# Another string of ordering rules for the planner of a fused attention and MLP kernel

## The chip, the cores and the metric

The kernel runs on one core of one Trainium2 chip. The metric is the device time in microseconds (us). A profile is one execution, recorded by the hardware profiler. A core has a matrix engine (TensorE, here PE; its weight loads are PEld), VectorE (DVE), ScalarE (ACT), GpSimd (POOL) and SyncE (SP), which issues DMAs. Each engine works through its own queue in order, and engines wait for each other by semaphores.

## The reference

All activations are bf16, with one batch, 2048 tokens of width 640, 32 query heads of width 20 that share one key and one value head, and an MLP of width 1728.

```python
xn = _layernorm(x, axis=-1)
q  = (xn @ wq).reshape(B, S, 32, 20).transpose(0, 2, 1, 3)
k, v = xn @ wk, xn @ wv
p  = softmax(einsum("bhqd,bkd->bhqk", q, k) * 20 ** -0.5)
A  = einsum("bhqk,bkd->bhqd", p, v).transpose(0, 2, 1, 3).reshape(B, S, 640) @ wo
out = x + A + silu(xn @ w1) @ w2
```

## The kernel before

**A planner writes the queues.** The program isn't written out by hand. `build` describes each instruction as an `Op` with its engine, an assumed duration (`occ`), what it reads and writes and a priority, and a greedy scheduler (`Sched`) then steps a clock for each engine. At each step the engine whose clock is lowest picks one of the ops that could start (`step_pe` for PE, `step_other` for the rest), and `commit` fixes it at the next place of that engine's queue. `emit` turns the resulting orders into instruction streams and adds the semaphore waits that the data need. Nothing of the planned times goes into the program, only the orders; but which bank of PSUM, which buffer and which engine an op uses is decided on the way too, so one other choice early changes everything that follows.

**Attention.** Heads are taken in eight groups of four and queries in four blocks of 512, which makes 32 head groups ("groups", `NGR`). For each group and each of the 16 tiles of 128 keys there are four blocks of scores of 128 x 512, one for each head, 2048 in all. The score matmuls (L1078) contract over only 20 of 128 rows, so up to four of them run side by side in four row strips of the array: a score set. A block fills one of the eight PSUM banks. Its exponential is taken in one of two ways:
- ACT takes two or three blocks at a time, from adjoining banks, with one instruction of 1024 or 1536 columns (L1166). `plan` chooses the banks and `make_s_act` makes the score set.
- DVE approximates it: L1409 adds a constant, clamps and converts to int16, which read as bf16 is a power of two that is linear between the powers. Two further copies of the tile, shifted by constants (the "shifts", four blocks at a time), smooth the result. They run on POOL (L1448) or on DVE (L1453), as `dve_advance` finds POOL loaded. Four blocks make a batch, opened by `claim`.

The product of p with v (p.v; L1201) runs as four column strips side by side, a set of four matmuls, and adds up in one PSUM bank for the group; a batch of DVE's has three sets, one for each shift. An extra column of v sums p. At the end of a group the bank is copied to U (L1250, or added to an earlier part, L1249), the sums are turned into reciprocals and spread by DMAs, POOL multiplies (L860) and DMAs pack the result into oT. The last two groups take a shorter way: sums by PE (L999), spread by PE (L1017), a product on DVE (L1026).

**The other matrix work ("misc").** `fill_misc` lists it in a fixed order: the q projections, the hidden layer of the MLP (h; its tanh is ACT's L773, its product DVE's L776), and for each query block the output jobs, which add the MLP's second layer and the attention's projection (out; for the last query block y, with a remainder fin). All of them run as sets of four column strips through `col_mm` (L447), 512 columns for q and h and 320 for out and y; a matmul of a job may instead run as one or four row strips beside a score set (`row_mm`, L454). PE can't run row strips and column strips at once, so it goes back and forth between bursts of scores and bursts of sets.

**What PE does next** is decided in `step_pe`: `pe_candidates` gathers what could start now (a score set for ACT "s", one for DVE "d", p.v from ACT "p" or from DVE "pd", misc "m" or "l", a row strip "r" and others), and the order of kinds is written as a list that depends on the mode that PE is in and on how far things lag. If nothing can start within 250 ns or so, `filler` puts in matmuls on zeros (L1725).

**The rules.** About thirty numbers steer these choices; they stand in `BASE` and are read as `ru.name`. `RULES` has one letter for each of some forty variants that change one or two of these numbers. `PLAN` is a string with one letter for each 10 us of PE's planned time:

```python
if sc.t["pe"] >= piece * PIECE:          # PIECE = 10000.0 ns
    ru.__dict__.update(BASE)
    ru.__dict__.update(RULES[rule(piece)])
    piece += 1
```

Some of the letters: `need` and `hold` (m, P, n, Q) say how long ahead of ACT's running dry a score set is placed and whether it waits for three adjoining banks; `stay` (o, J, K) lets PE go on with its sets until so many ns before ACT runs dry; `slack`, `want` (q, w, v) say when banks are kept for DVE; `open` (p, t) how many batches DVE may have open; `pj` (z, C, E) when a shift goes to POOL; `rows`, `half` (A, B, G, H, I) when matmuls run as row strips; `hold2` (x, F) whether a second misc job may hold a bank; `leadmax` (k, l) how far misc may run ahead of the attention; a changes nothing.

Of the kernel before, what the change touches and what calls it, by code (L numbers as in the profile page):

```python
# [105 lines left out]
RULES = dict(a={}, b=dict(keep=0.0), c=dict(lagp=3), d=dict(lagp=5), e=dict(lagp=0), f=dict(patience=200.0), g=dict(dwant=0.0),  # L106
             h=dict(zcap=4), i=dict(zcap=3), j=dict(homes=0), k=dict(leadmax=-1.0, lead=-1.0), l=dict(lead=0.08, leadmax=0.1),
             m=dict(need=740.0), n=dict(hold=0.0), o=dict(stay=640.0), p=dict(open=1), q=dict(slack=560.0), r=dict(hungry=1000.0), s=dict(claim=9), t=dict(open=3), u=dict(claim=4), v=dict(want=2), w=dict(slack=850.0), x=dict(hold2=4), y=dict(bnd=0), z=dict(pj=-1e9), A=dict(rows=0), B=dict(rows=2, rowmin=2), C=dict(pj=2000.0), D=dict(openlag=3), E=dict(pj=8000.0), F=dict(hold2=3), G=dict(rows=1), H=dict(half=0), I=dict(half=3), J=dict(stay=560.0), K=dict(stay=720.0), P=dict(need=560.0), Q=dict(hold=120.0), L=dict(uopen=3), M=dict(uopen=4), N=dict(uopen=5), O=dict(uopen=0))
PLAN = "acbtJKazNvhaJvxvixrrnrKzDDnQDmoqvknpfLBGvDPmoJdftFQdkttaQBBoknQEaoz"


def rule(n):
    return PLAN[n] if n < len(PLAN) else "a"
PACE = 1.0
# [2059 lines left out]
```

## Time and profile before

| | us |
|---|---|
| median of 3 runs | 691.98 |
| lowest and highest run | 691.73, 692.18 |
| the profiled execution | 691.7 |
| its span, first to last instruction | 689.9 |
| granted PE clock, mean | 1.00 |

The profile's page gives each engine's busy time as a share of the span. Views of the trace give busy time in stretches of the span, groups of instructions by line and shape (count | total busy, mean of one | idle time of the engine ahead of them, and what ended it), who waited for whom (total, times, longest), an engine's instructions in order of time (equal ones that follow each other are merged; the second number is how long the merged run lasted), and the chain of waits: the work that ended last, followed back from the last instruction. Ends of matmuls are modelled, so a busy PE may still have small gaps. L followed by a number is a line of the kernel. A count of matmuls is of single ones; four column strips make a set.

### The profile page before, as it was taken

To read this page: it belongs to the slowest core of one execution; us is meant where nothing else is said; L and a number is where in the kernel's file an instruction comes from. 1 tells how busy PE (TensorE), PEld (TensorE's weight loads), DVE (VectorE), ACT (ScalarE), POOL (GpSimd) and SP (SyncE) were. 2 spreads that over 40 slices of the span, in tenths; PEclk is the share of its full clock that TensorE was granted. 3 is DMA by queue.
4 is the path that set the end of the run, shared out by engine and by line. 5 is a ranking of instruction groups with operands and counts; after the bars stand their busy time and mean duration, and the time that the engine had idled before them with its cause. 6 is when DMAs were issued, how large, how long until landed. Compare 5 with 4: busy or idle time off the path is not lost.

```text
span 689.9 us, 22614 instructions
## 1 busy us (share of the span) xinstructions
PE 676.4 (98%) x9870; PEld 234.4 (34%) x9873; DVE 594.7 (86%) x1017; ACT 665.9 (97%) x726; POOL 583.9 (85%) x351
## 2 busy tenths in 40 slices
PE   8999999999999999999999999999999999999998
PEld 5432222322233333323233333322232333333345
DVE  7899989988998867898988888798988889989973
ACT  6999999999999999999999999999999999999990
POOL 6668899898988889898899899989889998888860
PEclk9999999999999999999999999999999999999999
DMA  7753221122221232321212223222222202223201
GB/s 217 178 180 42 20 20 15 33 35 30 18 28 12 31 40 30 69 34 17 33 14 30 29 31 40 23 65 29 29 19 22 22 18 32 31 23 68 23 7 41
DMA packets 34241, 28.97 MB, mean 42 GB/s; under 512 B 15486, under 2 KB 29662, under 8 KB 34142
## 3 DMA queue, kind: packets, MB, share of 16 engines
q1 hardware_dynamic: 33854, 27.20, 25.7%
q8 instruction: 77, 1.26, 0.8%
q10 hardware_dynamic: 288, 0.33, 0.1%
q14 instruction: 22, 0.18, 0.1%
HBM read 11.09 MB, written 2.62 MB: 20 GB/s over the span
## 4 chain that ended last, share of the span: by engine, by line
PE 76%; ACT 16%; DVE 4%; POOL 1%; SPq 1%; DMA 1%; issue 1%; DVEq 0%; ACTq 0%
PE psall L1201 26%; PE psall L1078 25%; PE psall L447 23%; ACT sbt L1166 14%; DVE sbt L1409 1%; ACT sbt L773 1%; POOL sbt L1448 1%; SPq L706 1%; DMA sbt<-sbt 0%; PE psall L621 0%; DVE sbt L563 0%; PE psall L734 0%; DVE sbt L607 0%; PE psall L1725 0%; DVE sbt L565 0%
## 5 line engine op out<-in xcount | busy, mean ns | idle before, releaser
L1166 ACT ACTIVATE sbt<-psall 128x1024 bf16<-128x1024 f32 (+1 forms) x654 | 643.0, 1156 | 2.3 <-PE psall L1078 2.1
L1448 POOL TENSOR_SCALAR sbt<-sbt 128x2048 int16<-128x2048 int16 x275 | 521.7, 1897 | 70.4 <-DVE sbt L1453 22.4
L1409 DVE TENSOR_SCALAR sbt<-psall 128x512 int16<-128x512 f32 x676 | 441.8, 685 | 64.4 <-PE psall L1078 60.1
L1078 PE MATMUL psall<-sbt 32*128 32x512 bf16 x2048 | 269.2, 384 | 4.3 <-ACT sbt L1166 1.6
L1201 PE MATMUL psall<-sbt 128*32 128x512 bf16 x3400 | 264.8, 384 | 0.6 <-POOL sbt L1448 0.4
L447 PE MATMUL psall<-sbt 128*32 128x320 bf16 (+3 forms) x3792 | 227.6, 332 | 2.5 <-DVE sbt L1409 0.8
L1078 PEld LDWEIGHTS psall<-sbt 32*128 32x128 bf16 x2048 | 71.4, 91 | 238.8 <-ACT sbt L1166 172.7
L447 PEld LDWEIGHTS psall<-sbt 128*32 128x32 bf16 (+1 forms) x3792 | 82.4, 95 | 82.7 <-issue 44.7
L1201 PEld LDWEIGHTS psall<-sbt 128*32 128x32 bf16 x3400 | 70.1, 94 | 114.5 <-issue 71.0
L1453 DVE TENSOR_SCALAR sbt<-sbt 128x2048 int16<-128x2048 int16 x63 | 48.6, 784 | 0.7 <-PE psall L1201 0.6
L860 POOL TENSOR_TENSOR sbt<-sbt 128x512 bf16<-128x512 f32 x30 | 38.2, 1274 | 7.2 <-DVE sbt L1453 5.5
L776 DVE SCALAR_TENSOR_TENSOR sbt<-sbt,psall 128x512 bf16<-128x512 bf16 x52 | 35.6, 684 | 5.2 <-ACT sbt L773 2.6
L773 ACT ACTIVATE sbt<-psall 128x512 bf16<-128x512 f32 x52 | 37.6, 723 | 0.1
L1250 DVE COPY sbt<-psall 128x512 f32<-128x512 f32 x31 | 21.2, 683 | 1.1 <-PE psall L1201 1.0
L454 PE MATMUL psall<-sbt 32*128 32x320 bf16 x70 | 21.3, 305 | 0.0
L1725 PE MATMUL psall<-sbt 128*32 128x256 bf16 (+1 forms) x228 | 14.4, 355 | 1.2 <-DVE sbt L487 1.2
L693 DVE TENSOR_SCALAR sbt<-psall 128x512 bf16<-128x512 f32 x20 | 13.6, 680 | 0.4 <-PE psall L447 0.4
L903 DVE SCALAR_TENSOR_TENSOR sbt<-psall,sbt 128x320 bf16<-128x320 f32 x24 | 11.6, 485 | 2.1 <-PE psall L447 1.6
L572 POOL TENSOR_TENSOR sbt<-sbt 128x2 f32<-128x2 f32 x8 | 5.7, 709 | 8.7 <-DVE sbt L570 8.3
L585 POOL TENSOR_SCALAR sbt<-sbt 128x640 bf16<-128x640 bf16 x12 | 10.4, 874 | 1.5 <-DVE sbt L577 1.5
L919 DVE SCALAR_TENSOR_TENSOR sbt<-psall,sbt 128x320 f32<-128x320 f32 x8 | 3.9, 486 | 8.0 <-PE psall L447 8.0
L1725 PEld LDWEIGHTS psall<-sbt 128*32 128x32 bf16 x228 | 7.0, 114 | 4.5 <-issue 1.6
(64 smaller groups left out, 117.9 us busy)
## 6 DMA issues: line engine op xcount, KB each, us to landing
sbt<-sbt SPq DMA_DIRECT2D x120, 64.0 KB, 3.9
sbt<-in_A_x_dram SPq DMA_DIRECT2D x28, 160.0 KB, 4.0
sbt<-sbt SPq DMA_DIRECT2D x213, 20.0 KB
out_dram<-sbt SPq DMA_DIRECT2D x14, 160.0 KB, 2.0
sbt<-in_B_w_dram SPq DMA_DIRECT2D x1, 2160.0 KB, 13.4
sbt<-in_B_w_dram SPq DMA_DIRECT2D x1, 2080.0 KB, 8.1
sbt<-sbt SPq DMA_DIRECT2D x75, 8.0 KB
sbt<-in_A_wq_dram SPq DMA_DIRECT2D x1, 800.0 KB, 5.9
```

The costliest lines, as they stand in the source:

```text
L447: ins = pe.matmul(ps[j * SLOT:(j + 1) * SLOT, b * BANK + off:b * BANK + off + n], w[:, j * SLOT:(j + 1) * SLOT], x, start=start, stop=stop ...
L454: return pe.matmul(ps[0:w.shape[-1], b * BANK:b * BANK + n], w[k], x[k], start=start, stop=stop, tile_position=(r * SLOT, 0))
L773: t = Op("act", lambda a: a.activation(t_buf[0:rows, ts, :], bk(job.bank, 0, QW, rows=rows), AF.Tanh, scale=0.5), t_act(512), ACT_END, pre ...
L776: u = Op("dve", lambda v: v.scalar_tensor_tensor(out=hT[par][0:rows, fk, :], in0=t_buf[0:rows, ts, :], scalar=1.0, in1=bk(job.bank, 0, QW, ...
L860: nm = pool(lambda e: e.tensor_tensor(oU[:, us, :], U_sb[:, us, :], Rrep, ALU.mult), 1356.0, POOL_END, pre=[uc] + lc + pack_op.get(divmod( ...
L1078: return pe.matmul(bk(b), kT_rep[i * SLOT:(i + 1) * SLOT, kt * P:(kt + 1) * P], qT[i * SLOT:(i + 1) * SLOT, g % NQ, :], start=True, stop=T ...
L1166: return a.activation(Ebuf[:, es * QW:es * QW + w], ps[:, buf[0] * BANK:buf[0] * BANK + w], AF.Exp, scale=ESCALE)
L1201: ins = pe.matmul(ps[i * SLOT:(i + 1) * SLOT, ub * BANK:ub * BANK + QW], lhsT, rhs, start=(first and k < HG), stop=(last and k >= len(lst) ...
L1409: p1 = Op("dve", lambda v: v.tensor_scalar(z16[:, i * QW:(i + 1) * QW], bk(job.bank), ZBIAS, 0.0, ALU.add, ALU.max), t_dve(QW) + 2.0, DVE_ ...
L1448: op = pool(lambda v, t=t, j=j, zin=zin: v.tensor_scalar(t.bitcast(I16), zin, float(SHIFT[j]), 1.0, ALU.add, ALU.mult), POOL_SHIFT, POOL_E ...
L1453: op = dve(lambda v, t=t, j=j, zin=zin: v.tensor_scalar_add(t.bitcast(I16), zin, float(SHIFT[j])), t_dve(N, 4), prio=SPRIO - 0.01 * j, **args)
L1725: ins = pe.matmul(ps[i * SLOT:(i + 1) * SLOT, ub * BANK:ub * BANK + n], zero_t[:, 0:SLOT], zero_t[:, 0:n], start=fresh, stop=fresh, tile_p ...
```

## The change

Only the string of letters changes. Its length stays 67, the first three letters stay, and of the other 64 two agree by place.

```diff
-PLAN = "acbtJKazNvhaJvxvixrrnrKzDDnQDmoqvknpfLBGvDPmoJdftFQdkttaQBBoknQEaoz"
+PLAN = "acbgxnoQpQJvpnaQodtxzpvEoQJBJoaodpJqQaDqJovpkBrnvxBxQJBfaaooHoatano"
```

Behind the first three letters the new string has o (stay=640) ten times, a (the base alone) seven times, Q (hold=120) and J (stay=560) six times each, p (open=1) five times, and x (hold2=4), n (hold=0), v (want=2) and B (rows=2, rowmin=2) four times each. The old one has v five times, t (open=3), a, n, D (openlag=3), Q and o four times each, and twenty other letters up to three times each. The planner runs with these while the program is built, so the change shows in the program as other orders in the queues and as other counts of a few kinds of instructions:

| | before | after |
|---|---|---|
| ACT L1166, 1024 / 1536 / 512 columns | 590 / 64 / 0 | 594 / 61 / 1 |
| DVE L1453, shifts | 63 | 65 |
| POOL L1448, shifts | 275 | 273 |
| DVE L1249, partial copies of U | 6 | 4 |
| PE L1725, matmuls on zeros | 228 | 188 |
| PE L447, 512 / 320 columns | 1476 / 2208 | 1468 / 2196 |
| PE L454, row strips | 70 | 78 |
| PE, bursts of one kind | 1322 | 1331 |

All other kinds have the same counts. The first instruction that stands elsewhere comes after about 30 us of the planned time; behind it every queue is ordered anew. PE's queue ends like this (a row is a run of equal matmuls):

```
before                         after
L1078 128x512 x3               L1078 128x512
L1201  32x512 x56              L454  128x320
L447   32x320 x80              L447   32x320 x36
L999  128x4   x4               L1201  32x512 x4
L1017  32x128 x16              L447   32x320 x72
L447   32x320 x68              L999  128x4   x4
                               L1017  32x128 x16
then in both: L447 32x128 x20, 32x384 x20, 32x128 x4, 32x384 x12, 32x128 x8,
32x384 x4, 32x128 x4, 32x512 x24, 32x256 x36, 32x512 x12
```

Ahead of that, ACT's queue ends with seven instructions of 1536 columns before, and with nine of 1536 and one of 512 after.

## The prediction

> **What bounds the kernel now.** I read the table of engines first, then busy time in six stretches of 100 us, then ACT's instructions, then the end of the chain of waits.
>
> ```profile
> span 689.9 us, 22614 instructions
> ...
> PE 676.4 (98%) x9870; PEld 234.4 (34%) x9873; DVE 594.7 (86%) x1017; ACT 665.9 (97%) x726; POOL 583.9 (85%) x351
> ```
> ```profile
> core 0: us, PE busy (x) PEld busy (x) DVE busy (x) ACT busy (x) POOL busy (x), PEclk, DMA share, GB/s
> ...
> 536.00:636.00 100.00, 99.47 (x1570) 35.00 (x1568) 90.10 (x148) 99.79 (x105) 88.03 (x51) 1.00 0.25 34
> sum 600.00, PE 593.90 PEld 191.89 DVE 527.98 ACT 599.32 POOL 532.86; mean PE 98.98 PEld 31.98 DVE 88.00 ACT 99.89 POOL 88.81
> ```
>
> Two engines are full at once. From 36 to 636 us ACT lacks 0.7 us of being always busy and PE 6.1 us. To see which sets the end, I take ACT's own pace and compare it with the stage.
>
> ```profile
> L1166 ACT ACTIVATE sbt<-psall 128x1024 bf16<-128x1024 f32 x590 | 563.9, 1118 | 2.3 <-PE psall L1078 2.1
> ...
> L1166 ACT ACTIVATE sbt<-psall 128x1536 bf16<-128x1536 f32 x64 | 95.1, 1509 | 0.0
> ```
> ```profile
> 13.59 1.92 ACT L1166 ACTIVATE sbt<-psall 128x1024 bf16<-128x1024 f32 x2
> ...
> 22.64 7.44 ACT L1166 ACTIVATE sbt<-psall 128x1024 bf16<-128x1024 f32 x8 [0.48 <-PE psall L1078]
> 29.88 0.69 ACT L631 ACTIVATE sbt<-psall 128x512 bf16<-128x512 f32 x1
> ...
> 664.06 9.52 ACT L1166 ACTIVATE sbt<-psall 128x1536 bf16<-128x1536 f32 x7
> ```
>
> Eight exponentials of two banks start at 22.64 and the next instruction at 29.88: 0.905 us each, although one lasts 1.118 (neighbours overlap by 0.21). Seven of three banks end 9.52 us after the first starts: without that overlap 1.33 each. The difference, 0.427, is one bank; one bank alone takes 0.905 - 0.427 = 0.48. So ACT needs 590 x 0.905 + 64 x 1.33 + 57 x 0.48 = 646.5 us (57 one-bank instructions at L773, L744 and L631, by the program). It had from 13.59 to 664.06 + 9.52 = 673.58: 660.0 us. Only 13.5 us, 2%, are stalls. The time is therefore the 13.6 us ahead, ACT's work with its stalls, and the 16.3 us from the last exponential to the end. PE comes next: what it hasn't finished when ACT ends is paid for one to one in those 16.3 us.
>
> ```profile
> 662.06 0.55 PE psall L1201 x8
> ...
> 664.72 0.98 PE psall L1201 x16
> ...
> 671.11 0.33 PE psall L1078 x3
> 671.43 3.21 PE psall L1201 x56
> 674.65 2.72 PE psall L447 x80
> 677.36 0.98 PE psall L999 x8
> 678.35 1.01 PE psall L1017 x32
> 679.36 6.60 PE psall L447 x200
> ```
>
> This is the end of the chain. Four column matmuls run side by side as one set. Sixteen against eight of L1201 give (0.98 - 0.55) / 2 = 0.215 us for a set of 512 columns, and 0.55 - 2 x 0.215 = 0.12 for the change of mode before a burst. Eighty of L447 give 2.72 / 20 = 0.136 for a set of 320. After the last score set (671.11) PE still has 14 sets of p.v, 20 sets of 320 columns, the sums and spreads of the last head group, and 200 matmuls more: PE ends with a backlog.
>
> **The change part by part.** The work stays the same; the string picks other rules for 62 of 67 pieces of 10 us of planned time, all from 30 us on, and the planner lays the queues anew. I counted both programs' instructions in queue order and priced the differences.
>
> ACT: 594 exponentials of two banks for 590, 61 of three for 64, one of one bank for none; 1372 blocks of scores in both, and 169 batches for DVE in both. 4 x 0.905 - 3 x 1.33 + 0.48 = **+0.1 us**.
>
> DVE and POOL: two shifts of z move from POOL (275 to 273) to DVE (63 to 65), and two partial copies of U fall away (6 to 4).
>
> ```profile
> L1453 DVE TENSOR_SCALAR sbt<-sbt 128x2048 int16<-128x2048 int16 x63 | 48.6, 784 | 0.7 <-PE psall L1201 0.6
> ```
> ```profile
> 672.30 1.90 POOL L1448 TENSOR_SCALAR sbt<-sbt 128x2048 int16<-128x2048 int16 x1 [2.04 <-PE psall L1201]
> ```
>
> POOL has 2 x 1.90 = 3.8 us less to do, DVE at most 2 x 0.784 = 1.6 us more. Both lie under ACT, whose share of the span is 97% against their 86 and 85%; I cost them at nothing. Without that cover DVE's part would be 1.6.
>
> PE's order at the end, which decides: after the last score set the new queue holds 1 set of p.v for 14. Of 320 columns it holds 9 sets ahead of that p.v, 18 between it and L999, and none behind L1017; before these were 0, 20 and 17 (68 of the 200). What follows (the final products, their DVE sums, two stores) is the same list. The tail from the last exponential's end is then, against 16.3: p.v 674.65 - 673.58 = 1.07 becomes one set and its hand-over, 0.3 (-0.8); two sets of 320 fewer (-0.3); 17 fewer (-2.3). Sum **-3.4 us**. The 17 sets also covered the way from L1017 over DVE's product to the first matmul that needs it. Ten other sets (128 and 384 columns, by width 5 x 0.05 + 5 x 0.16 = 1.1 us) still stand there; DVE's two products were through 0.5 us after L1017, so I cost the lost cover at nothing:
>
> ```profile
> 678.99 0.86 DVE L1026 TENSOR_TENSOR sbt<-sbt,psall 128x256 bf16<-128x256 f32 x2 [0.40 <-PE psall L1017]
> ```
>
> This has to be earned earlier: 13 x 0.215 + 10 x 0.136 = 4.2 us more PE work stands before the last score set. Its sources: PE's fill matmuls, which compute nothing, go from 21 sets to 11 behind the prologue.
>
> ```profile
> 521.65 0.60 PE L1725 MATMUL psall<-sbt 128*32 128x512 bf16 x8
> ...
> 530.70 0.28 PE L1725 MATMUL psall<-sbt 128*32 128x256 bf16 x4
> ```
>
> Between these two stand nine bursts of fill, ten sets: the old order has nothing else for PE there, while its tail holds work. The new order has three sets left in the last third of the run. Eight sets of 512 and two of 256 fewer free 8 x 0.215 + 2 x 0.11 (half of it) = 1.9 us. The last score set may also come later, because its exponential has one bank and not three: 1.33 - 0.48 = 0.85, with the 0.1 above 0.95. Nine more bursts cost 9 x 0.12 = 1.1; five more sets (two of 512, three of 320) done as row matmuls inside score sets save 0.8. So 4.2 - 1.9 - 0.95 + 0.3 = **1.6 us** must come out of PE's 6.1 us of idle time. Bounds: if all comes from idle time it costs nothing; if none does, ACT's stalls grow by 1.6. I take the middle, +0.8, since some idle time is waiting for banks that ACT holds. Burst by burst the orders look alike: after 30 us, 60 stretches from one exponential's scores to the next hold over 0.2 us more PE work than the exponential before them lasts; in the new order 45. I see no reason for more stalls, and allow 1.5 us either way (a tenth of the 13.5).
>
> Sum against the profiled execution, 691.7 (span 689.9 and 1.8 around it): +0.1 - 3.4 + 0.8 = -2.5, so 689.2. The median is 0.3 higher (691.98): **689.5 us**, own range 687.2 to 691.8 (0.8 and 1.5 to either side).
>
> [...]
>
> **The rivals.**
>
> ```profile
> PEld psall L1078 <- ACT sbt L1166: 172.7, 479, 0.8
> ...
> PEld psall L1201 <- POOL sbt L1448: 12.5, 49, 0.5
> ```
>
> (a) *No denser.* Score loads wait 479 times for ACT's banks; where PE waits so, work can't be packed more tightly, and more work between score sets only makes ACT wait. For: PE is busy for 99.5 of the 100 us from 536 on. Against: 1.9 us are fills, visibly free. Its price: stalls rise by a quarter, 3.4 us, and the tail's gain is given back: 691.98 + 0.1 - 3.4 + 3.4 = 692.1, no change.
>
> (b) *POOL late at the end; slower.* By the row above, POOL's last shift ends at 674.2, 0.6 us after the last exponential, and the last p.v sets wait for it. In the new order every p.v set from DVE's batches stands ahead of the last score set, so that shift must end some 2 us before the last exponential does. If it comes as it did, 2.6 us late, PE stands with the last score set behind it; one shift more makes 2.6 + 1.9 = 4.5: 689.5 + 4.5 = 694.0. It is slower than before from that second shift on. For: p.v waits for POOL 49 times even now. Against: POOL has 3.8 us less to do, and nine three-bank exponentials end the new order (seven before), so DVE's last batch is some 2.7 us earlier.
>
> (c) *The clock falls.* With ten fill sets fewer a gap in PE's work could slow its clock. Ten us at half speed would lose 5: 694.5. For: the ten sets filled holes of the old order one by one. Against: no row shows a clock below 1.00, and the longest wait of the score loads is 0.8 us.
>
> **How the numbers follow.** Forecast 0.66, a gain beyond 687.2 another 0.03, (a) 0.15, (b) 0.14, (c) 0.02. What a measurement can tell from no change is about 0.2%, 1.4 us: under 690.6 and over 693.4. Of the forecast's 0.66 I put 0.60 under 690.6. Faster: 0.60 + 0.03 = 0.63; same: 0.06 + 0.15 = 0.21; slower: 0.14 + 0.02 = 0.16. The range goes from 687.2 to 692.7, which takes in (a) with 0.6 above it; (b) and (c) are left out.
>
> **What would show it.** Right: ACT's last exponential still ends at 673.6 to 675 us, about 13 us before the end; behind the last score set one p.v set, and no 320-column run between L1017 and the final products; fewer L1725 and PE idle time of 4 to 5 us between 36 and 636. Wrong: a last exponential past 676 (stalls took the gain); L1201 waiting for L1448 over a microsecond near 670; a clock under 1.00; PE idle between L1017 and the final products.

## The result, and the profile after

| | before | after |
|---|---|---|
| median, 20 executions each (us) | 691.82 | 689.70 |
| lowest and highest | 691.38, 692.51 | 689.52, 692.44 |
| the profiled execution | 691.7 | 690.16 |
| its span | 689.9 | 688.3 |
| last exponential of ACT ends at | 673.58 | 675.10 |
| from there to the end | 16.3 | 13.2 |

The ratio of the times is 0.9972 (95% interval 0.9966 to 0.9979): 0.28% faster. The forecast was 689.5. The profiled execution of the changed kernel is 0.5 us above its median, so the sums below, which go by the two profiles, come to less (690.16 - 691.7 = -1.5) than the medians (-2.1).

The table of engines, busy time in one long stretch (36 to 636 us: PE, PEld, DVE, ACT and POOL in this order, then PE's clock) and ACT's instructions by shape, all of the changed kernel:

```profile
span 688.3 us, 22511 instructions
...
PE 675.7 (98%) x9821; PEld 232.2 (34%) x9821; DVE 591.3 (86%) x1017; ACT 666.4 (97%) x728; POOL 581.7 (85%) x349
```
```profile
36.00:636.00 600.00, 593.62 (x8461) 191.16 (x8463) 531.23 (x871) 598.58 (x654) 527.06 (x289) 1.00 0.25 33
```
```profile
L1166 ACT ACTIVATE sbt<-psall 128x1024 bf16<-128x1024 f32 x594 | 563.5, 1100 | 2.6 <-PE psall L1078 2.5
...
L1166 ACT ACTIVATE sbt<-psall 128x1536 bf16<-128x1536 f32 x61 | 89.7, 1512 | 0.6 <-PE psall L1078 0.6
...
L1166 ACT ACTIVATE sbt<-psall 128x512 bf16<-128x512 f32 x1 | 0.7, 700 | 0.0
```

PE's idle time from 36 to 636 us is 6.4 us, where it was 6.1: it has *not* been used. ACT's own work by the prediction's prices is 594 x 0.905 + 61 x 1.33 + 58 x 0.48 = 646.5, against 646.4 before. Now ACT's queue in order of time, its beginning and its end:

```profile
13.64 1.92 ACT L1166 ACTIVATE sbt<-psall 128x1024 bf16<-128x1024 f32 x2
...
654.95 20.15 ACT L1166 ACTIVATE sbt<-psall 128x1024 bf16<-128x1024 f32 x18 [0.30 <-PE psall L1078]
675.64 0.66 ACT L1302 ACTIVATE sbt<-psall 128x256 f32<-128x256 f32 x2 [0.54 <-PE psall L1201]
```

The exponentials run from 13.64 to 654.95 + 20.15 = 675.10, 661.5 us; less the 646.5 of own work, 14.9 us are stalls, with unrounded terms, where the same sum gave 13.6 before. The stage is 1.5 us longer (1.4 of stalls, 0.1 of own work), and what follows it 3.1 us shorter. The end of the chain of waits shows why it is shorter:

```profile
672.38 0.25 PE psall L1078
672.62 0.01 issue
672.63 0.86 PE psall L447 x20
673.50 0.23 PE psall L1201 x4
673.72 0.24 PE psall L1078
673.97 1.41 PE psall L447 x36
675.38 0.21 PE psall L1201 x4
675.59 2.44 PE psall L447 x72
678.03 0.99 PE psall L999 x8
679.02 1.01 PE psall L1017 x32
680.03 4.29 PE psall L447 x132
684.32 0.02 issue
684.35 1.34 DVE sbt L967 x2
```

Read it from the last exponential's end, 675.10. One p.v set is done at 675.59 (before, 1.07 us after the exponential, now 0.49); 18 sets of 320 columns take 2.44 (2.72); sums and spread the same; then 132 matmuls in 4.29 where 200 took 6.60. That is -0.58 - 0.28 - 2.31 = -3.2, and the tail of the span is 13.2 against 16.3.

### The profile page after: what moved, and what is told of

It reads as the page before. It is cut to its first block, busy times and chain, and to the rows that moved or that the text cites. A ratio compares the mean times of both kernels' runs of the same rounds, so it can differ in the third digit from the quotient of the medians.

```text
span 688.3 us, 22511 instructions
## 1 busy us (share of the span) xinstructions
PE 675.7 (98%) x9821; PEld 232.2 (34%) x9821; DVE 591.3 (86%) x1017; ACT 666.4 (97%) x728; POOL 581.7 (85%) x349
## 4 chain that ended last, share of the span: by engine, by line
ACT 52%; PE 42%; DVE 3%; POOL 1%; DMA 0%; issue 0%; DVEq 0%; ACTq 0%
ACT sbt L1166 48%; PE psall L1201 14%; PE psall L1078 14%; PE psall L447 13%; ACT sbt L773 3%; DVE sbt L1409 2%; POOL sbt L1448 1%; PE psall L595 1%; PE psall L621 1%; DVE sbt L1453 0%; DMA sbt<-in_A_x_dram 0%; PE psall L999 0%; PE psall L1017 0%; ACT sbt L554 0%; DVE sbt L565 0%
## 5 line engine op out<-in xcount | busy, mean ns | idle before, releaser
L1166 ACT ACTIVATE sbt<-psall 128x1024 bf16<-128x1024 f32 (+1 forms) x656 | 640.0, 1138 | 3.2 <-PE psall L1078 3.0
L1448 POOL TENSOR_SCALAR sbt<-sbt 128x2048 int16<-128x2048 int16 x273 | 518.6, 1900 | 72.5 <-PE psall L1201 15.3
L447 PE MATMUL psall<-sbt 128*32 128x320 bf16 (+2 forms) x3772 | 225.9, 332 | 2.1 <-DVE sbt L776 0.7
L447 PEld LDWEIGHTS psall<-sbt 128*32 128x32 bf16 x3772 | 80.4, 95 | 85.5 <-issue 45.4
L1201 PEld LDWEIGHTS psall<-sbt 128*32 128x32 bf16 x3400 | 68.8, 94 | 115.5 <-issue 71.9
L1453 DVE TENSOR_SCALAR sbt<-sbt 128x2048 int16<-128x2048 int16 x65 | 47.6, 750 | 0.0
L773 ACT ACTIVATE sbt<-psall 128x512 bf16<-128x512 f32 x52 | 34.9, 671 | 0.2 <-PE psall L447 0.2
L454 PE MATMUL psall<-sbt 32*128 32x320 bf16 (+1 forms) x78 | 24.4, 313 | 0.0
L1725 PE MATMUL psall<-sbt 128*32 128x256 bf16 (+1 forms) x188 | 11.1, 375 | 1.2 <-DVE sbt L487 1.2
L563 DVE BATCH_NORM_STATS2 sbt<-sbt 128x6 f32<-128x320 bf16 x14 | 6.6, 472 | 2.0 <-DMA sbt<-in_A_x_dram 2.0
```

The costliest lines, as they stand in the source:

```text
L447: ins = pe.matmul(ps[j * SLOT:(j + 1) * SLOT, b * BANK + off:b * BANK + off + n], w[:, j * SLOT:(j + 1) * SLOT], x, start=start, stop=stop ...
L454: return pe.matmul(ps[0:w.shape[-1], b * BANK:b * BANK + n], w[k], x[k], start=start, stop=stop, tile_position=(r * SLOT, 0))
L773: t = Op("act", lambda a: a.activation(t_buf[0:rows, ts, :], bk(job.bank, 0, QW, rows=rows), AF.Tanh, scale=0.5), t_act(512), ACT_END, pre ...
L1166: return a.activation(Ebuf[:, es * QW:es * QW + w], ps[:, buf[0] * BANK:buf[0] * BANK + w], AF.Exp, scale=ESCALE)
L1201: ins = pe.matmul(ps[i * SLOT:(i + 1) * SLOT, ub * BANK:ub * BANK + QW], lhsT, rhs, start=(first and k < HG), stop=(last and k >= len(lst) ...
L1448: op = pool(lambda v, t=t, j=j, zin=zin: v.tensor_scalar(t.bitcast(I16), zin, float(SHIFT[j]), 1.0, ALU.add, ALU.mult), POOL_SHIFT, POOL_E ...
```

## The experiments

Each changes the queues after the planner has written them, or takes another string. Their times are compared with runs of the kernel before on the same chip; the changed kernel was run once more with the last group, and where it wasn't run on the same chip, differences from it are taken by way of the kernel before (-2.1 us, in its repeat -1.9). The helpers are:

```diff
+def leave_out(sc, gone):     # take ops out of PE's queue; their waits pass to the next op,
+                             # and who waited for them waits for the op ahead of them
+def zero_set(sc, op):        # a set of four 512-column matmuls on zeros that adds
+                             # zero to the bank that p.v set `op` writes
...
         sc, dma_sems, sem = build(nc, A_x, A_wq, A_wk, A_wv, A_wo, B_x, B_w1, B_w2, out, stack)
+        tweak(sc)
         run = emit(nc, sc, dma_sems, sem)
```

### Is the tail paid one to one?

First, the kernel before with a short tail. It leaves out part of the last head group's p.v and part of the last output job.

```diff
+def tweak(sc):
+    pe = sc.order["pe"]
+    end = max(i for i, op in enumerate(pe) if op.mode == "s" and op.name.startswith("S"))
+    pv = [op for op in pe[end + 1:] if op.name.startswith("PV")]
+    spread = max(i for i, op in enumerate(pe) if op.name.startswith("spread"))
+    y = [op for op in pe[spread + 1:] if op.name.startswith("y")]
+    leave_out(sc, pv[:-1] + y[1:-1])
```

> The kernel before, with 13 of the 14 p.v sets that stand after its last score set left out, and 15 of the 17 sets of 320 columns behind the spread (L1017). Everything ahead of the last score set is untouched. Theory (what stands after the last exponential is paid one to one, 16.3 us of tail): 15 x 0.136 = 2.0 and the p.v sets after the last exponential 0.8, so 2.8 us faster than before (689.0), tail 13.5 us, last exponential's end unmoved at 673.6. Rival (PE is the bound everywhere, each set costs its price): 15 x 0.136 + 13 x 0.215 = 4.8 us faster. Second rival (the tail is held by DVE and DMA latencies, not by PE's sets): under 1.5 us faster.

Measured: 691.02 against 691.57, ratio 0.9989 (0.9980 to 0.9997), only 0.6 us faster, and the last exponential ends at 673.44, unmoved. But the executions fall in two groups: two at 689.4 with a mean clock of 1.000, nine from 690.7 to 691.4 with 0.997 or 0.998. PE's instructions in order of time, and busy time in stretches of 2 us (the column behind POOL is the clock), in a profile of the second group:

```profile
670.90 0.39 PE L1078 MATMUL psall<-sbt 32*128 32x512 bf16 x3
673.54 0.40 PE L1201 MATMUL psall<-sbt 128*32 128x512 bf16 x4 [2.25 <-ACT sbt L1166]
673.76 4.58 PE L447 MATMUL psall<-sbt 128*32 128x320 bf16 x80
```
```profile
672.00:674.00 2.00, 0.46 (x12) 0.37 (x16) 0.00 (x0) 1.46 (x3) 1.29 (x1) 1.00 0.00 0
674.00:676.00 2.00, 2.00 (x49) 1.52 (x44) 0.49 (x1) 0.65 (x2) 0.00 (x0) 0.69 0.04 8
676.00:678.00 2.00, 2.00 (x36) 1.32 (x28) 0.00 (x0) 0.00 (x0) 0.00 (x0) 0.50 0.00 0
678.00:680.00 2.00, 2.00 (x44) 1.72 (x40) 0.95 (x4) 0.00 (x0) 0.00 (x0) 0.96 0.00 0
```

PE comes back at 673.54 from 2.25 us with nothing to do, and its clock is 0.69 on average from 674 to 676 and 0.50 from 676 to 678: the 80 matmuls that took 2.72 us in the chain of waits take 4.40 there (from the p.v set's end, 673.54 + 0.40 = 673.94, to 673.76 + 4.58 = 678.34). That is the prediction's rival of the clock, here in earnest, and it goes with the experiment's own hole: without the hole, in the next run, six clocks of six are 0.999 or 1.000. The two undisturbed executions are 2.2 us faster than before, where 2.8 was expected. The same without the hole leaves the p.v sets in:

```diff
-    leave_out(sc, pv[:-1] + y[1:-1])
+    leave_out(sc, y[1:-1])
```

> The kernel before, with only the 15 middle sets of 320 columns behind the spread left out; the 14 p.v sets after the last score set stay, so PE doesn't stand idle before the last exponential ends. Theory (the tail is paid one to one; the run above lost part of its gain to the clock, which fell to half for some microseconds after PE's 2.3 us of idle time): 15 x 0.136 = 2.0 us faster than before, and a clock of 1.00 at the end in nearly all executions. Rival (the tail's sets are worth less than their price whatever the clock does): 0.5 to 1 us faster.

Measured: 689.95 against 691.80, ratio 0.9971 (0.9959 to 0.9982): 1.85 us faster, all six clocks 0.999 or 1.000, the last exponential at 673.44 and 14.8 us of tail. The sets behind the spread are paid at nearly their price. The end of the chain of waits shows what is missing from it:

```profile
678.21 0.62 PE psall L1017 x16
678.83 0.02 issue
678.85 0.42 DVE sbt L1026
679.27 0.01 issue
679.29 0.43 DVE sbt L1026
679.72 0.04 issue
679.76 4.49 PE psall L447 x132
```

From L1017 to PE's end it is 6.04 us, where the 7.61 of before less the 2.04 left out would be 5.57: with so little behind the spread, PE waits about 0.5 us for DVE's product. The run with the hole has the same wait, which accounts for most of what the two undisturbed executions lack. In the changed kernel nothing waits there, although it has no such set left. By the two programs, the first final product of the kernel before writes a bank that the spread has filled, and so has to wait until L1026 has read it; in the changed kernel it writes the bank of the last output job.

Now the other way, the changed kernel with a long tail:

```diff
+    pv = next(op for op in pe[end + 1:] if op.name.startswith("PV"))
+    pe[end + 1:end + 1] = [zero_set(sc, pv) for _ in range(14)]
```

> The changed kernel, with 14 sets of 512 columns on zeros put behind its last score set (3.0 us of PE work; they add zero to the open bank). Theory: paid one to one, 2.9 to 3.0 us slower than the changed kernel, 0.9 us slower than before (692.6); last exponential unmoved. Second rival (latencies hold the tail): under 1.5 us slower than the changed kernel.

Measured: 693.13, ratio to before 1.0024 (1.0015 to 1.0034). By way of the kernel before it is 3.5 to 3.7 us slower than the changed kernel. The last exponential stays within 0.15 us (675.25), and the tail is 16.5 for 13.2. The chain of waits shows where the 3.4 come from, the 56 added matmuls and a row strip behind them that in the changed kernel runs beside its last score set:

```profile
674.19 3.13 PE psall L2122 x56
677.33 0.24 PE psall L454
```

So sets in the tail are paid nearly one to one both ways, and the 3.1 us that the change took from the tail are its gain, of which the stage gives back about 1.

### What does PE's work cost ahead of the last score set?

The changed kernel, with sets left out of the stage, or with sets of zeros added to it. Leaving out means that the MLP and the projections lack these terms.

```diff
+    mid = [op for op in pe[900:end] if op.mode == "p" and op.name[0] in "hoqy" and op.job is not None
+           and op.job.dyn and op.ends == (False, False)]
+    leave_out(sc, [mid[k * len(mid) // n] for k in range(n)])            # n = 30, then 150
...
+    pv = [op for op in pe[900:-150] if op.name.startswith("PV")]
+    ok = [a for a, b in zip(pv, pv[1:]) if a.writes[-1] is b.writes[-1]
+          and a.name.split("_")[0].strip("PVd") == b.name.split("_")[0].strip("PVd")]
+    for op in [ok[k * len(ok) // 20] for k in range(20)]:
+        pe.insert(pe.index(op) + 1, zero_set(sc, op))
```

> The changed kernel, with 30 sets of misc work (middle ones of their jobs, spread evenly over the stage from 60 us or so to the last score set) left out: 30 sets of 512 or 320 columns, 4.8 us of PE work by the price of a set. Tells where the extra stalls of ACT in the changed kernel (15.8 against 14.4 us in the two profiled executions) come from. Theory (the extra PE work packed into the stage makes ACT wait): ACT's stalls fall by 1 to 2 us, 1 to 2 us faster than the changed kernel. Rival (PE the bound everywhere): 4.8 us faster. Rival (ACT's stalls come from how banks turn over, not from PE's load): within 0.4 us of the changed kernel.

(The stalls in this expectation, 15.8 and 14.4, are 0.8 to 0.9 above what the sum used here gives, 14.9 and 13.6; their difference is the same.)

> The changed kernel, with 150 misc sets left out of the stage, 23 us of PE work or 3.4%. Theory (ACT sets the stage; 30 sets fewer gained 0.1 us): within 1.5 us of the changed kernel, ACT's stalls still over 13 us; with so much idle time the clock may fall in places and then it is slower by 1 to 3 us. Rival (PE the bound everywhere): over 15 us faster.

> The changed kernel, with 20 sets of 512 columns on zeros put behind p.v sets evenly over the stage (4.3 us of PE work more ahead of the last score set, about what the change moved there). Theory (PE has 6 us of idle time and takes some of it): 1 to 2 us slower than the changed kernel. Rival (PE the bound everywhere): 4.3 us slower. Rival (bank turnover, PE has room): within 0.4 us.

| changed kernel with | us | same chip's before | ratio to before (95%) | against the changed kernel's -2.1 (its repeat: -1.9) |
|---|---|---|---|---|
| 30 sets fewer | 689.48 | 691.57 | 0.9971 (0.9960 to 0.9982) | 0.0 (-0.2) |
| 150 sets fewer | 689.12 | 691.80 | 0.9962 (0.9949 to 0.9975) | -0.6 (-0.8) |
| 20 sets more | 692.23 | 691.57 | 1.0009 (1.0000 to 1.0018) | +2.8 (+2.6) |

Each interval is 0.6 to 0.9 us either way. Less work for PE buys little. Busy time from 36 to 636 us with 150 sets fewer shows what happens to it:

```profile
36.00:636.00 600.00, 585.03 (x7921) 179.39 (x7919) 532.18 (x873) 598.54 (x655) 527.09 (x290) 1.00 0.25 33
```

PE is shown idle for 15.0 us instead of 6.4, and ACT is as full as ever, 598.5 for 598.6. The 540 matmuls that are missing from the stretch are worth about 20 us of PE work, so more than half of the time they free isn't shown as idle: the idle time of the trace is less than PE's room. ACT's stalls in that profile are 13.9 us, 1.0 less. So about 14 of the 14.9 us of stalls stay even with 23 us less work for PE.

Whether the 1.4 us of stalls that the change added come from the denser work is not settled. The times with 30 sets fewer speak against it. The traces speak for it in part. From the start of ACT's first exponential to that of one and the same later instruction of its queue, near 650 us, it is 637.2 to 637.3 us in four profiles that have the changed kernel's order there, 636.5 with 30 sets fewer, 636.2 with 150 fewer and 639.8 with 20 more. Twenty sets more (4.3 us) cost 2.7 us in all, six tenths of their price: the stage stands at the edge, where taking work away gains little and adding it costs.

In one of seven executions with 30 sets fewer, the profiled one, the clock fell again (690.9 us), to 0.90, 0.50 and 0.75 in the three stretches of 2 us from 660 on, behind the sums of the group before last and with PE shown idle for only 0.15 us from 658 to 662 (the third number from the end is the clock):

```profile
658.00:660.00 2.00, 2.00 (x25) 1.09 (x17) 1.83 (x5) 2.00 (x4) 1.92 (x2) 1.00 0.09 23
660.00:662.00 2.00, 1.85 (x28) 0.99 (x31) 1.20 (x3) 2.00 (x3) 1.92 (x2) 0.90 0.04 10
662.00:664.00 2.00, 2.00 (x28) 0.69 (x24) 0.92 (x2) 1.57 (x2) 1.37 (x2) 0.50 0.00 0
664.00:666.00 2.00, 2.00 (x43) 1.01 (x39) 0.00 (x0) 1.25 (x2) 1.92 (x2) 0.75 0.00 0
```

One of the five executions with 150 sets fewer has a mean clock of 0.997 too, at 690.01 us; its trace wasn't kept.

### POOL late at the end

The changed kernel, with POOL's last shift done twice.

```diff
+    pool = sc.order["pool"]
+    op = [o for o in pool if o.name.startswith("s")][-1]
+    again = Op("pool", op.fn, op.occ)
+    again.deps = set()
+    pool.insert(pool.index(op), again)
+    again.deps, op.deps = op.deps, {again}
```

> The changed kernel, with POOL's last shift done twice (the same values written twice), so that its result is 1.9 us later. Measures the prediction's rival of a late POOL: the last shift ended at 671.5 in the profile, and the last p.v sets of DVE's batches begin at 671.9. Theory (PE takes its queue in order, so the last two score sets wait behind that p.v set): 1.9 less the 0.4 of margin, 1.5 us slower than the changed kernel, with L1201 waiting for L1448 over 1 us and ACT's last exponential later by as much. Rival (PE has other work between, or the bank of the p.v sets is not what the score sets wait for): within 0.4 us.

Measured: 691.32 against 691.49 before and 689.58 for the changed kernel: 1.7 us slower than the latter, nearly its whole gain (ratio to before 0.9999, 0.9990 to 1.0008). PE's instructions in order of time:

```profile
671.47 0.32 PE L447 MATMUL psall<-sbt 128*32 128x320 bf16 x4
673.42 0.61 PE L1201 MATMUL psall<-sbt 128*32 128x512 bf16 x8 [1.63 <-POOL sbt L1448]
673.97 0.39 PE L1078 MATMUL psall<-sbt 32*128 32x512 bf16 x3
```

The p.v set waits 1.63 us for the shift, the score set stands behind it, and ACT's last exponential ends at 676.35 for 675.00; the tail is 13.7 us for 13.2. In the changed kernel itself POOL's queue ends like this:

```profile
663.68 7.84 POOL L1448 TENSOR_SCALAR sbt<-sbt 128x2048 int16<-128x2048 int16 x4 [0.63 <-DVE sbt L1453]
```

The last shift is done at 671.52, 0.4 us before PE needs it (671.93). The rival's mechanism is real; in this execution it missed by 0.4 us.

### Other strings

> Another string: the changed one's first 62 letters, then the old one's last 5. The queues are the changed kernel's but for the last 50 us. By the sum of the prediction: ACT's work as in the changed kernel, the same stalls but for the end, and after the last exponential 17 sets of 320 columns for 18, none behind the spread: 0.1 us from the changed kernel, so 2.0 us faster than before. Rival (only the whole string as grown holds the gain): within 0.5 us of before.

```diff
-PLAN = "acbgxnoQpQJvpnaQodtxzpvEoQJBJoaodpJqQaDqJovpkBrnvxBxQJBfaaooHoatano"
+PLAN = "acbgxnoQpQJvpnaQodtxzpvEoQJBJoaodpJqQaDqJovpkBrnvxBxQJBfaaooHoQEaoz"
```

> Another string: the old one's first 35 letters, then the changed one's last 32. ACT gets 570 exponentials of two banks and 84 of three, 20 blocks of scores more, because DVE gets 164 batches for 169; the tail is much shorter (6 p.v sets, no set of 320, two of the five final products already begun). By the sum of the prediction: ACT's work -20 x 0.905 + 20 x 1.33 = +8.5 us, tail about 9.9 for 16.3 us = -6.4, so 2.1 us slower than before if the stalls stay as they are. Rival (a short tail is what counts): 6 us faster. Second rival (PE's total is what counts; fills are 28 sets for 21, the rest alike): within 1.5 us of before.

```diff
-PLAN = "acbtJKazNvhaJvxvixrrnrKzDDnQDmoqvknpfLBGvDPmoJdftFQdkttaQBBoknQEaoz"
+PLAN = "acbtJKazNvhaJvxvixrrnrKzDDnQDmoqvknqQaDqJovpkBrnvxBxQJBfaaooHoatano"
```

> A string grown from the changed one by further changes of single letters (five letters differ: Q for the tenth old J and others at the end). ACT: 592 exponentials of two banks, 64 of three: -2 x 0.905 + 3 x 1.33 - 0.48 = +1.7 us against the changed kernel. Tail: 2 p.v sets and 17 sets of 320 columns after the last score set for 1 and 27, of which 4 for 18 behind the last p.v: about -1.5 us, since the copy of U then leaves PE some 0.6 us idle. Sum of the prediction: 0.2 us slower than the changed kernel (689.9), between 689.3 and 690.5 by the stalls. Rival (what was gained in the planner's own clock is gained on the chip): 0.3 us faster than the changed kernel.

```diff
-PLAN = "acbgxnoQpQJvpnaQodtxzpvEoQJBJoaodpJqQaDqJovpkBrnvxBxQJBfaaooHoatano"
+PLAN = "acbgxnoQpQdvpnaQodtxzpvEoQJBJoGodpJqQaDqJovpkBrnvxBxQJBfaDooHoltAiB"
```

(The last one differs in seven letters, where its expectation counts five.) The three, with the terms of the sum from each profile:

| | own work of ACT | stalls | tail | median | its before | ratio (95%) |
|---|---|---|---|---|---|---|
| before | 646.4 | 13.6 | 16.3 | 691.82 | | |
| changed | 646.5 | 14.9 | 13.2 | 689.70 | 691.82 | 0.9972 (0.9966 to 0.9979) |
| changed, again | 646.5 | 14.9 | 13.2 | 689.58 | 691.49 | 0.9972 (0.9962 to 0.9982) |
| s1, last 5 letters old | 646.5 | 14.8 | 13.0 | 689.70 | 691.80 | 0.9969 (0.9956 to 0.9981) |
| s2, first 35 letters old | 654.9 | 15.8 | 10.3 | 695.83 | 691.80 | 1.0057 (1.0043 to 1.0071) |
| s3, grown on | 648.2 | 14.1 | 11.4 | 689.18 | 691.49 | 0.9967 (0.9955 to 0.9979) |

s1 came out as summed. s2 has the shortest tail and is the slowest: ACT's eight and a half microseconds more own work outweigh six of tail, and 2.2 us more stalls came on top, which the sum had not (4.0 us slower than before, where it gave 2.1). For s3 the sum gave 0.2 us slower than the changed kernel and missed the wrong way: own work is +1.7 as summed, but the tail is -1.8 for -1.5, and stalls are lower, by 0.8 in the profiles and by 0.3 by the medians. It is the fastest of all, 0.4 us under the changed kernel, which is the number that its rival gave (what was gained in the planner's own clock is gained on the chip); no run tests the planner's clock further. Its executions (689.07 to 689.38) lie wholly under the changed kernel's of the same chip (689.46 to 689.97).

## Why the prediction was right

The forecast of 689.5 lies 0.2 us from the median. That is closer than the sum was: it gave a difference of -2.5 us and -2.1 came, but it was laid on a median of 691.98 from 3 runs, which 20 runs put at 691.82.

**ACT sets the stage, +0.1.** Right. Own work is 646.5 against 646.4, and taking 3.4% of PE's work away gained 0.6 to 0.8 us.

**The tail, -3.4.** Right in kind and nearly in size: -3.1. The last p.v set came 0.49 us after the exponential, where 0.3 was allowed; PE was still in the nine sets ahead of it when the exponential ended.

**The lost cover behind the spread, nothing.** Right: the 132 matmuls follow L1017 without a gap. The reason given, ten other sets that still stand there, isn't the whole of it. The kernel before with its sets left out has the same ten and waits 0.5 us. That the changed kernel doesn't is owed to the bank that its first final product writes, which the prediction didn't look at.

**PE has to earn 4.2 us, of which 1.6 come from idle time, half of it turning into stalls (+0.8).** The size was near (stalls +1.4 in the profiles; by the medians, -2.1 - 0.1 + 3.1 leaves +0.9) but the account was wrong. Nothing came from the idle time that the trace shows, which went from 6.1 to 6.4 us, where 4 to 5 had been named as a sign of being right. The last score set came not 0.95 but 2.6 us later (671.11 to 673.72), and with the 1.9 us of fills this pays for the 4.2 and the 0.3 of extra bursts (bursts of row strips and of column strips take turns in the traces; with POOL late, for one, column sets start at 673.42, the next score set at 673.97 and column sets again at 674.29). In the prediction's own terms this lies near its other bound, nothing from idle time and 1.6 us of stalls; the +0.8 was the middle of two bounds, chosen and not read from a row, and that it fits the medians is partly luck. How much of the added stalls is the price of denser work stays open: with 30 sets fewer, more than what was moved, the time stays, but the trace is 0.7 us ahead at 650 us. By the order of time some stalls are single score sets that waited for their banks; from 249 to 254 us, ACT's queue in the changed kernel:

```profile
248.16 4.39 ACT L1166 ACTIVATE sbt<-psall 128x1024 bf16<-128x1024 f32 x4
253.15 1.45 ACT L1166 ACTIVATE sbt<-psall 128x1536 bf16<-128x1536 f32 x1 [0.60 <-PE psall L1078]
```

What decides how many of these an order has wasn't settled. The five strings have 13.6 to 15.8 us of stalls, and the one count made ahead, 60 crowded stretches against 45, pointed the other way. That s3 has fewer of them than the sum took is about half of why its sum came out 0.6 us too slow.

**Rival (a), no denser.** It didn't happen, and its reason is half true: 20 sets more in the stage cost six tenths of their price.

**Rival (b), POOL late.** It didn't happen by 0.4 us; the measured price of one shift too late is 1.7 us, where 1.9 less a margin was expected.

**Rival (c), the clock.** Nearly absent: 19 of 20 executions have 0.999 or 1.000. One has 0.998 and 692.44 us, 2.7 above the median, more than the 1.6 us that the fall in the short tail cost; its trace wasn't kept, so where its clock fell is not known. No run shows the rival's ten us at half speed: by the clock's means, the two falls that traces show lack 1.70 us of full speed each. In 57 executions of the kernel before beside the experiments no clock is under 0.999.

## What to carry to other kernels

Where two engines look full, ask which of them the time follows: find one engine's bare cadence, subtract its own work from the stage, and then take work from the other engine; here leaving out 23 us of TensorE's work gained under 1 us inside the stage (adding 4.3 us cost 2.7), while sets behind its end cost or saved nearly their price (3.0 us added cost 3.5 to 3.7, 2.0 left out saved 1.85), but for a wait on another engine that they had covered (0.5 us). A greedy planner's order can be judged ahead of a run by three sums read from the queue (the bounding engine's own work, what is left for the others when it ends, and how late the last hand-over may be), but not its stalls, which here move the time by a microsecond or two either way. A backlog at the end costs its length, but here the matrix engine's clock also stayed up with it: a mean of 0.999 or 1.000 in six executions of six with 14 p.v sets in the tail, 0.997 or 0.998 in nine of eleven with one.

## What the runs showed of the hardware that wasn't expected

After a hole of 2.25 us in TensorE's work (the kernel before with a short tail) its clock fell to half: on average it was 1.00 from 672 to 674, 0.69 from 674 to 676, 0.50 from 676 to 678, 0.96 from 678 to 680 and 1.00 again from 680 to 682. Over these stretches the means lack 2 x (0.31 + 0.50 + 0.04) = 1.70 us of full speed. So it went in 9 of 11 executions and not in the other two, which are 1.6 us faster; the trace of one of the nine shows it, and the mean clocks of the others (0.997 or 0.998) fit it. With the p.v sets left in, so without the hole, all six executions have 0.999 or 1.000. Why two of the eleven kept their clock, no run shows. The other fall seen, in one execution with 30 sets fewer, had no such hole ahead of it: PE is shown idle for 0.15 us from 658 to 662, and the means of 0.90, 0.50 and 0.75 from 660 to 666 lack 1.70 us as well. The kernel's own 4-column sums (L999) stand there, in two bursts that begin at 658.87 and 659.73; whether they bring it about wasn't tried.
